# Two decode layers with a key and value cache: every cache load as two halves of 64 partitions, on two DMA queues

## The chip, the cores and the metric

The kernel runs on one core of a Trainium2 chip. The metric is the device time of one execution in microseconds (us); smaller is better. A difference of under about 0.2% (some 5 us) can't be told from no change here.

## What is computed

The reference takes one token for each of two sequences (x is 2 x 1 x 576) through attention, a gated MLP, attention and the MLP again, with the same weights and the same cache both times, all in float32. There are 32 heads of 128 dimensions and 8192 cached positions.

```python
def _A_ref(x, k_cache, v_cache, wq, wo):
    q = (x @ wq).reshape(B, Sq, H, Dh).transpose(0, 2, 1, 3)
    scores = jnp.einsum("bhqd,bhkd->bhqk", q, k_cache) * (Dh ** -0.5)
    p = _softmax(scores, axis=-1)
    o = jnp.einsum("bhqk,bhkd->bhqd", p, v_cache)
    return o.transpose(0, 2, 1, 3).reshape(B, Sq, H * Dh) @ wo
def _B_ref(x, w_gate, w_up, w_down):
    return (_gelu(x @ w_gate) * (x @ w_up)) @ w_down
x = x + _A_ref(_layernorm(x), k_cache, v_cache, wq, wo)
x = x + _B_ref(_layernorm(x), w_gate, w_up, w_down)
x = x + _A_ref(_layernorm(x), k_cache, v_cache, wq, wo)
x = x + _B_ref(_layernorm(x), w_gate, w_up, w_down)
```

Each head's keys are 4 MB, and so are its values. For 2 sequences and 32 heads that is 537 MB in a layer, nearly all of which is read from DRAM twice, once for each layer. This is far more than the weights.

## The kernel before, in words

The attention of a layer goes item by item. An item is two heads of one sequence (30 items, `PAIRS`), or at the end of the list a single head (4 items, `SINGLE`). A load of the keys or values of a pair is 8 MB: 128 partitions with 128 cached rows, that is 64 KB in one run, each. Partitions 0 to 63 hold the first head of the pair and 64 to 127 the second. Layer 0 takes the items from first to last and layer 1 from last to first, so that what is still held from the end of layer 0 need not be loaded again.

The tile `space` is most of the on-chip memory. `Arena` is its planner: six slots of 32 KB a partition, so places for three pairs, and behind them a ring of four smaller places for weights. All loads stand in one list, in the order of `plan_first`, `plan_mlp` and `plan_second`. A load is written into the program as soon as its place is free there: `done` frees a place and calls `pump`, which issues from the head of the list. So the order of the loads is fixed, and each DMA instruction waits at its place in its engine's program until the last reader of the memory is done. Keys and values alternate: keys of item n+1, values of item n.

All cache loads but two go through `load` (line 165), which issues one DMA on SP's queue (L168). `cache`, `half`, `one` and `several_parts` call it. `by_rows` (L233) and all loads of weights (L257 to L322) issue their DMAs on SP themselves. ScalarE issues eight small loads of x at the start (L143), and one of the two stores at the end (L1201).

Work on an item's keys: VectorE multiplies them with the query (L743), GpSimd adds the halves of each row (L772), and VectorE sums them into scores (L775). VectorE and TensorE find the peak (L799 to L809), and ScalarE computes the weights (L824, L832). Work on the values: TensorE multiplies them with the weights (L913), except for the last two parts, which VectorE weighs (L880) and GpSimd folds (L883) before TensorE adds them in (L891). The place of an item's keys is freed by L775, that of its values by L913 and, last, L891. TensorE broadcasts the next item's query (L658) once VectorE has begun on the present one, and ScalarE scales a pair's result (L955). At the start of layer 1 ScalarE also copies queries (L740), so that GpSimd can multiply some rows (L759), and sums some rows itself (L765). L615 is the products with `wq`.

Of the kernel before, what the change touches and what calls it, by code (L numbers as in the profile page):

```python
# [15 lines left out]
P = 128  # L16
# [8 lines left out]
JC = 16  # L25
# [37 lines left out]
ITEMS = [Item(b, h, 2) for h in range(0, H - 2, 2) for b in range(B)]  # L63
# [62 lines left out]
def decode_layers(ctx, tc, x_in, kc, vc, wq, wo, wg, wu, wd, out):  # L126
    nc = tc.nc
# [12 lines left out]
    for c in range(4):  # L140
        for s in range(2):
            lo = 32 * c + s * B
# [16 lines left out]
    def part_at(at, n):  # L159
        return space[:, at:at + n]  # L160
# [4 lines left out]
    def load(at, n, src, lo, hi):  # L165

        t = part_at(at, (hi - lo) * PART).rearrange("p (j d) -> p j d", d=DH)
        nc.sync.dma_start(t, ITEMS[n].source(src)[:, lo * JC:hi * JC, :])  # L168

    def cache(key, src, n, slots=None):  # L170

        parts = ITEMS[n].parts

        def make():
            at = arena.pair(key) if slots is None else arena.slots(key, slots, parts)
            if at is None:
                return False
            load(at[0], n, src, 0, parts)
            ready[key] = dict(enumerate(map(part, at)))
            places[key] = at  # L180
            return True

        queue.append(make)

    def half(key, src, n, k, slot):

        def make():
            at = arena.slots(key, (slot,), 4, k)
            if at is None:
                return False  # L190
            load(at[0], n, src, k, k + 4)
            ready.setdefault(key, {}).update((k + i, part(a)) for i, a in enumerate(at))
            return True

        queue.append(make)

    def one(key, src, n, k, where):

        def make():
            at = arena.ring((key, k), PART) if where is None else arena.take((key, k), places[where[0]][where[1]], PART)  # L200
            if at is None:
                return False
            load(at, n, src, k, k + 1)
            ready.setdefault(key, {})[k] = part(at)
            return True

        queue.append(make)
# [250 lines left out]
    for b in range(B):  # L458
        rows = ident.rearrange("p (c v i r) -> p i r v c", c=4, v=4, i=2)[:, :, :, b, :]
# [769 lines left out]
```

## Time and profile before

| | |
|---|---|
| Median of 3 runs | 2681.43 us (2681.32 to 2682.24) |
| The profiled execution: its own time | 2681.31 us |
| Its span in the profile | 2679.5 us |
| Bytes read from DRAM | 1152.39 MB |
| VectorE busy | 1992.6 us (74%) |
| GpSimd busy | 1560.5 us (58%) |
| TensorE busy | 880.8 us (33%) |
| ScalarE busy | 165.7 us (6%) |
| SP's DMA queue, share of 16 DMA engines | 99.8% |

In the profile SP's queue is q1 and ScalarE's is q10. "SPq" and "ACTq" are the issuing instructions of SP and ScalarE, in which an engine spends its time only until the DMA is handed over. L numbers are lines of the kernel before; after the change lines behind 168 are two higher.

### The profile page before, as it was taken

The page shows a single profiled execution, that of the slowest core. Times are in us where ns is not written, and L with a number is a line of the kernel's source. Part 1 is how long each engine was busy: PE and PEld are TensorE (multiplying, and loading weights), DVE is VectorE, ACT ScalarE, POOL GpSimd, SP SyncE. Part 2 cuts the span into 40 slices and gives each one's busy share as a digit, 9 for nine tenths or more (in the row PEclk, how much of TensorE's full clock was granted, in tenths as well). Part 3 has the DMA queues.
Part 4 walks back from the last instruction along what each step waited for, and adds up shares of the span by engine and source line. Part 5 has one row for each costly group of instructions (what it writes and reads, how often), then busy time and mean ns, then how long its engine had stood idle before and what let it go on. Part 6 is the DMA issues. An engine that isn't in the chain of part 4 may idle for free.

```text
span 2679.5 us, 15405 instructions
## 1 busy us (share of the span) xinstructions
PE 880.8 (33%) x6198; PEld 268.7 (10%) x6198; DVE 1992.6 (74%) x907; ACT 165.7 (6%) x792; POOL 1560.5 (58%) x411
## 2 busy tenths in 40 slices
PE   1313332232223233334663323223222323332346
PEld 0000000000000000011221000000000000000022
DVE  4877888888788888867038778888888888888740
ACT  0000000000000000001026000000000000000000
POOL 2546676667667666744028457666766666676620
PEclk8666655665665566566986665566566556655678
DMA  9999999999999999999999999999999999999998
GB/s 423 437 429 434 436 434 432 431 436 433 431 434 434 434 433 432 436 428 427 417 417 431 436 433 434 434 430 434 435 432 432 436 434 433 431 437 434 428 430 385
DMA packets 29207, 1153.39 MB, mean 430 GB/s; under 512 B 3256, under 2 KB 3280, under 8 KB 4048
## 3 DMA queue, kind: packets, MB, share of 16 engines
q1 hardware_dynamic: 29096, 1152.40, 99.8%
q8 instruction: 48, 0.79, 0.1%
q14 instruction: 23, 0.19, 0.0%
q10 hardware_dynamic: 40, 0.01, 0.0%
HBM read 1152.39 MB, written 0.00 MB: 430 GB/s over the span
## 4 chain that ended last, share of the span: by engine, by line
DMA 67%; DVE 19%; PE 8%; POOL 2%; ACT 2%; issue 1%; another core or an unknown queue 0%; SPq 0%; POOLq 0%; ACTq 0%; DVEq 0%
DMA space<-in_A_k_cache_dram 59%; DVE space L743 17%; PE acc L891 3%; DMA space<-in_B_w_down_dram 2%; DMA space<-in_B_w_gate_dram 2%; POOL space L772 2%; DVE scores L775 2%; PE bank L658 1%; DMA space<-in_A_v_cache_dram 1%; DMA space<-in_B_w_up_dram 1%; PE bank L809 1%; ACT prz L832 1%; PE acc L913 1%; DMA space<-in_A_wo_dram 1%; PE bank L845 1%
## 5 line engine op out<-in xcount | busy, mean ns | idle before, releaser
L772 POOL TENSOR_TENSOR space<-space 128x3072 f32<-128x3072 f32 (+4 forms) x221 | 1128.4, 5106 | 459.1 <-DVE space L743 330.7
L743 DVE TENSOR_TENSOR space<-space,bank 128x6144 f32<-128x6144 f32 (+4 forms) x223 | 1111.9, 4987 | 344.7 <-DMA space<-in_A_k_cache_dram 273.7
L775 DVE TENSOR_REDUCE scores<-space 128x48 f32<-128x3072 f32 (+4 forms) x223 | 568.7, 2550 | 92.1 <-POOL space L772 92.1
L913 PE MATMUL acc<-space,prz 128*16 128x512 f32 (+1 forms) x3312 | 510.1, 780 | 357.9 <-DMA space<-in_A_v_cache_dram 346.4
L883 POOL TENSOR_TENSOR space<-space 128x2048 f32<-128x2048 f32 x147 | 398.0, 2708 | 392.3 <-DVE space L880 376.8
L658 PE MATMUL bank<-qsb,few 4*64 4x128 f32 (+1 forms) x256 | 46.1, 436 | 894.8 <-DVE space L743 887.1
L880 DVE TENSOR_TENSOR space<-space,bank 128x4096 f32<-128x4096 f32 x49 | 216.6, 4421 | 1.7
L913 PEld LDWEIGHTS acc<-space,prz 128*16 128x16 f32 (+1 forms) x3312 | 108.7, 117 | 742.0 <-issue 449.7
L824 ACT ACTIVATE nbs<-bank 128x2 f32<-128x2 f32 (+1 forms) x68 | 11.6, 171 | 2010.4 <-PE bank L809 1957.1
L658 PEld LDWEIGHTS bank<-qsb,few 4*64 4x64 f32 (+1 forms) x256 | 20.6, 201 | 914.2 <-DVE space L743 897.4
L580 POOL TENSOR_TENSOR rstd<-ve,few 128x1 f32<-128x1 f32 x4 | 2.2, 551 | 171.3 <-DVE ve L578 171.3
L891 PE MATMUL acc<-space,few 128*16 128x512 f32 x98 | 92.6, 1048 | 0.0
L801 PE MATMUL bank<-ident,m 128*1 128x128 f32 x68 | 20.7, 305 | 196.1 <-DVE m L799 195.9
L936 PE MATMUL bank<-few,wide 128*32 128x4 f32 (+1 forms) x272 | 20.9, 200 | 170.1 <-DVE wide L928 170.1
L1153 DVE STREAM_TRANSPOSE gu<-acc 128x288 f32<-128x288 f32 x4 | 1.9, 484 | 92.6 <-ACT acc L1151 92.6
L832 ACT ACTIVATE prz<-scores,nbs 64x128 f32<-64x128 f32 (+1 forms) x128 | 50.7, 396 | 11.7 <-POOL prz L822 8.9
L765 ACT ACTIVATE space<-space 128x128 f32<-128x128 f32 x164 | 48.4, 297 | 19.5 <-DVE space L743 16.5
L809 PE MATMUL bank<-m,few 1*128 1x2 f32 (+1 forms) x136 | 39.0, 353 | 28.1 <-DVE m L807 28.1
L584 DVE TENSOR_TENSOR x<-bank,x 128x144 f32<-128x144 f32 x4 | 1.2, 308 | 59.4 <-PE bank L1186 39.7
L927 DVE TENSOR_TENSOR acc<-acc,few 128x512 f32<-128x512 f32 x34 | 23.5, 691 | 29.2 <-PE acc L913 29.2
L936 PEld LDWEIGHTS bank<-few,wide 128*32 128x32 f32 x272 | 19.1, 154 | 216.0 <-issue 211.0
L955 ACT ACTIVATE oT<-bank,rinv 32x8 f32<-32x8 f32 x108 | 28.1, 260 | 190.1 <-PE bank L936 189.1
(105 smaller groups left out, 495.8 us busy)
## 6 DMA issues: line engine op xcount, KB each, us to landing
space<-in_A_v_cache_dram SPq DMA_DIRECT2D x7, 4096.0 KB
space<-in_A_k_cache_dram SPq DMA_DIRECT2D x6, 4096.0 KB
space<-in_B_w_gate_dram SPq DMA_DIRECT2D x9, 1152.0 KB
space<-in_B_w_up_dram SPq DMA_DIRECT2D x9, 1152.0 KB
space<-in_B_w_down_dram SPq DMA_DIRECT2D x8, 1152.0 KB
space<-in_A_wq_dram SPq DMA_DIRECT2D x9, 1024.0 KB
space<-in_A_wo_dram SPq DMA_DIRECT2D x2, 4608.0 KB
space<-in_A_k_cache_dram SPq DMA_DIRECT2D x4, 2048.0 KB
```

The lines of the kernel that those rows point to most:

```text
L658: nc.tensor.matmul(qb[n][to, :], pick[32 * c:32 * c + 4, r:r + 1].to_broadcast([4, P // it.heads]), qsb[32 * c:32 * c + 4, (h % 4) * DH:(h ...
L743: nc.vector.tensor_tensor(out=u[:, :r, :], in0=t[:, :r, :], in1=qb[n].unsqueeze(1).to_broadcast([P, r, DH]), op=ALU.mult)
L765: nc.scalar.activation(u[:, j, :], u[:, j, :], AF.Copy, accum_out=S[n][:, base(n, k) + j:base(n, k) + j + 1])
L772: nc.gpsimd.tensor_tensor(out=half, in0=half, in1=u[:, :r, DH // 2:], op=ALU.add)
L775: nc.vector.tensor_reduce(out=S[n][:, base(n, k):base(n, k) + own_rows(n, k, m)], in_=prod.pop((n, k)), axis=AX.X, op=ALU.add)
L809: nc.tensor.matmul(mT[n][:, :heads], ones[0:1, :], m1[:, :heads], start=True, stop=True)
L832: nc.scalar.activation(pr[at, lo:].rearrange("p (g e) -> p g e", e=4)[:, 0:it.rows // 2 * it.heads:2 * it.heads, :], s[at, :it.rows].rearr ...
L880: nc.vector.tensor_tensor(out=t, in0=t, in1=share.unsqueeze(2).to_broadcast([P, rows, DH]), op=ALU.mult)
L883: nc.gpsimd.tensor_tensor(out=t[:, :rows - less], in0=t[:, :rows - less], in1=t[:, less:rows], op=ALU.add)
L891: nc.tensor.matmul(accumulator(n)[0:16, :], owner[:, 8 * ITEMS[n].b:8 * ITEMS[n].b + 16], part_at(arena.live[key, lo][0], 4 * DH), start=F ...
L913: nc.tensor.matmul(accumulator(n)[32 * c:32 * c + m, :], pr[:, at:at + m], t[g // 4][:, g % 4 * 4:g % 4 * 4 + 4, :].rearrange("p j d -> p ...
L936: nc.tensor.matmul(po[lo:lo + 32, i, :c], t[:, i::GH], of[:, :c], start=True, stop=True)
```

## The change

```diff
     def load(at, n, src, lo, hi):

         t = part_at(at, (hi - lo) * PART).rearrange("p (j d) -> p j d", d=DH)
-        nc.sync.dma_start(t, ITEMS[n].source(src)[:, lo * JC:hi * JC, :])
+        rows = ITEMS[n].source(src)[:, lo * JC:hi * JC, :]
+        for engine, p in ((nc.sync, 0), (nc.scalar, P // 2)):
+            engine.dma_start(t[p:p + P // 2], rows[p:p + P // 2])
```

Each of the 141 loads that go through `load` becomes two DMAs: partitions 0 to 63 on SP's queue and partitions 64 to 127 on ScalarE's. Both wait for the same readers of the place, each in its own engine's program. `by_rows` and the weights stay as they were.

At the start ScalarE's program before, behind its loads of x, had the table load, the scaled queries (`qsb`) and then the first items' softmax (`nbs`, `prz`):

```order
L143 DMA x<-in_A_x_dram 2x144 x8
L989 ACT_TABLE_LOAD
L989 ACTIVATE qsb<-acc,rstd 128x256 x2
L824 ACTIVATE nbs<-bank_124 128x2
L832 ACTIVATE prz,few<-scores,nbs 64x32x4 x2
```

Now it reads, at the same place:

```order
L143 DMA x<-in_A_x_dram 2x144 x8
L170 DMA space<-in_A_k_cache_dram 64x16384 x2
L170 DMA space<-in_A_v_cache_dram 64x16384
L991 ACT_TABLE_LOAD
L991 ACTIVATE qsb<-acc,rstd 128x256 x2
L170 DMA space<-in_A_k_cache_dram 64x16384
L826 ACTIVATE nbs<-bank_125 128x2
L834 ACTIVATE prz,few<-scores,nbs 64x32x4 x2
```

Three halves of loads stand ahead of `qsb`, the first of which waits for no reader.

In the middle of a layer, ScalarE's program for two items (`oT` is the scaled result of a pair) was:

```order
L824 ACTIVATE nbs<-bank_124 128x2
L832 ACTIVATE prz,few<-scores,nbs 64x32x4 x2
L824 ACTIVATE nbs<-bank_124 128x2
L832 ACTIVATE prz,few<-scores,nbs 64x32x4 x2
L955 ACTIVATE oT<-bank_124,rinv 32x8 x4
```

and is now:

```order
L826 ACTIVATE nbs<-bank_125 128x2
L834 ACTIVATE prz,few<-scores,nbs 64x32x4 x2
L170 DMA space<-in_A_k_cache_dram 64x16384
L170 DMA space<-in_A_v_cache_dram 64x16384
L826 ACTIVATE nbs<-bank_125 128x2
L834 ACTIVATE prz,few<-scores,nbs 64x32x4 x2
L170 DMA space<-in_A_k_cache_dram 64x16384
L957 ACTIVATE oT<-bank_125,rinv 32x8 x4
L170 DMA space<-in_A_v_cache_dram 64x16384
```

The halves stand between an item's weights and the next item's.

At the start of layer 1, where ScalarE computes more, it had, from the scaled queries on:

```order
L989 ACTIVATE qsb<-acc,rstd 128x256 x2
L740 COPY qs<-bank 128x128
L765 ACTIVATE space,scores<-space 128x128 x12
L730 COPY space<-prz 128x264
L765 ACTIVATE space,scores<-space 128x128 x12
```

and has now:

```order
L991 ACTIVATE qsb<-acc,rstd 128x256 x2
L170 DMA space<-in_A_k_cache_dram 64x2048
L742 COPY qs<-bank 128x128
L767 ACTIVATE space,scores<-space 128x128 x12
L732 COPY space<-prz 128x264
L767 ACTIVATE space,scores<-space 128x128 x7
L170 DMA space<-in_A_k_cache_dram 64x4096
L767 ACTIVATE space,scores<-space 128x128 x5
L170 DMA space<-in_A_k_cache_dram 64x2048 x2
```

Here halves of small loads stand ahead of the copy of the query, and within ScalarE's sums.

## The prediction

> **What bounds the kernel now.** I read the page from the top: the span, the forty slices, the queues, the chain of work that ended last.
>
> ```profile
> span 2679.5 us, 15405 instructions
> GB/s 423 437 429 434 436 434 432 431 436 433 431 434 434 434 433 432 436 428 427 417 417 431 436 433 434 434 430 434 435 432 432 436 434 433 431 437 434 428 430 385
> DMA packets 29207, 1153.39 MB, mean 430 GB/s; under 512 B 3256, under 2 KB 3280, under 8 KB 4048
> q1 hardware_dynamic: 29096, 1152.40, 99.8%
> q10 hardware_dynamic: 40, 0.01, 0.0%
> DMA 67%; DVE 19%; PE 8%; POOL 2%; ACT 2%; issue 1%; another core or an unknown queue 0%; SPq 0%; POOLq 0%; ACTq 0%; DVEq 0%
> ```
>
> The reader is to see that most slices stand at 430 to 437 GB/s and that one queue, q1, keeps the 16 DMA engines busy for 99.8% of the span. The chain shows DMA for 67% and VectorE for 19%, but the queue is full during VectorE's share too: VectorE sits in the chain only because it frees the place of a later load. The two attention stages alone, in a table of busy time by stage (last columns: granted clock, DMA share, GB/s):
>
> ```profile
> 24.00:1253.00 1229.00, 364.94 (x2077) 103.87 (x2081) 985.27 (x380) 57.12 (x228) 767.44 (x181) 0.60 1.00 433
> 1463.00:2576.00 1113.00, 328.25 (x1858) 91.95 (x1858) 909.70 (x347) 48.14 (x202) 724.79 (x169) 0.59 1.00 433
> ```
>
> Both run at 433 GB/s with a DMA share of 1.00. So the time is bytes divided by rate, and only two things can move it: a change of the rate, or a moment in which the queue runs dry. How near it is to dry, the chain in order of time and SP's issues show:
>
> ```profile
> 461.99 29.05 DMA space<-in_A_k_cache_dram
> 491.04 0.02 issue
> 491.07 6.57 DVE space L743
> ```
>
> ```profile
> 442.25 0.33 SPq L168 DMA_DIRECT2D space<-in_A_v_cache_dram  x1
> 461.99 0.33 SPq L168 DMA_DIRECT2D space<-in_A_k_cache_dram  x1
> 482.20 0.33 SPq L168 DMA_DIRECT2D space<-in_A_v_cache_dram  x1
> ```
>
> A pair's load is 128 partitions of 64 KB, 8.39 MB, and takes 8.39 / 0.433 = 19.4 us. The keys issued at 461.99 land at 491.04, 29.05 us later, so they stood 9.7 us behind the load before them. The values issued at 482.20 start when these keys have landed, 8.8 us later. **The lead is about 9 us.**
>
> **The change, part by part.** What goes through `load` is taken from the table of DMA issues, whose sizes are in KB:
>
> ```profile
> space<-in_A_v_cache_dram SPq DMA_DIRECT2D x7, 4096.0 KB
> space<-in_A_k_cache_dram SPq DMA_DIRECT2D x6, 4096.0 KB
> space<-in_A_k_cache_dram SPq DMA_DIRECT2D x4, 2048.0 KB
> space<-in_A_v_cache_dram SPq DMA_DIRECT2D x2, 2048.0 KB
> space<-in_A_k_cache_dram SPq DMA_DIRECT2D x4, 1024.0 KB
> space<-in_A_v_cache_dram SPq DMA_DIRECT2D x1, 3072.0 KB
> space<-in_A_v_cache_dram SPq DMA_DIRECT2D x1, 1024.0 KB
> space<-in_A_k_cache_dram SPq DMA_DIRECT2D x58
> space<-in_A_v_cache_dram SPq DMA_DIRECT2D x58
> ```
>
> The last two rows carry no size; they are the 116 pair loads, 973.1 MB by the shapes in the code. The others are 54.5 + 12.6 + 8.4 = 75.5 MB. Together 141 loads move 1048.6 MB, which at 433 GB/s is **2422 us**. The rest of the queue's 1152.40 MB, and the two ends of the kernel, are not touched.
>
> *Issue.* 141 DMAs more are issued, all on ScalarE. SP's cost 0.33 us each by the rows above; the only ones that ScalarE issues in a row are those of x:
>
> ```profile
> 1.04 14.66 ACTq L143 DMA_DIRECT2D x<-in_A_x_dram  x8
> ```
>
> That is 1.83 us each, waits included, so 47 to 258 us of ScalarE's time. ScalarE is busy for 165.7 us and waits for most of the rest, as its largest wait shows:
>
> ```profile
> ACT nbs L824 <- PE bank L809: 1957.1, 63, 41.0
> ```
>
> I cost the issues at nothing: ScalarE's 1957 us of waiting and the lead of 9 us hide them. If that cover were gone, a half would land up to 1.5 us late.
>
> *Waits.* In the middle of a layer the halves stand in ScalarE's program in the order in which SP issued them among ScalarE's own work:
>
> ```profile
> 460.18 0.17 ACT L824 ACTIVATE nbs<-bank 128x2 f32<-128x2 f32 x1 [37.49 <-PE bank L809]
> 461.19 0.18 ACT L832 ACTIVATION_READ_ACCUMULATOR prz<-scores,nbs 64x1 f32 x1
> 468.37 1.08 ACT L955 ACTIVATE oT<-bank,rinv 32x8 f32<-32x8 f32 x4 [6.99 <-PE bank L936]
> ```
>
> The softmax ends at 461.37 and the keys are issued at 461.99. The scaled result follows at 468.37, the values at 482.20. No half waits behind ScalarE's work, nor does that work wait behind a half: nothing.
>
> At the start of layer 1 this does not hold:
>
> ```profile
> 1382.31 0.27 ACT L740 COPY qs<-bank 128x128 f32<-128x128 f32 x1 [0.43 <-PE bank L658]
> 1382.65 2.51 POOL L759 TENSOR_TENSOR space<-space,qs 128x512 f32<-128x512 f32 x2 [11.62 <-ACT qs L740]
> 1388.40 9.19 SPq L168 DMA_DIRECT2D space<-in_A_k_cache_dram  x4
> 1394.24 0.75 DVE L775 TENSOR_REDUCE scores<-space 128x9 f32<-128x576 f32 x1 [2.58 <-POOL space L772]
> ```
>
> SP issues at 1388.40 the load whose second half now stands ahead of the copy at 1382.31. So the copy comes 6.1 us later, GpSimd's L759 with it, and VectorE's L775, which frees the next places. If the queue has 6 us of work, the cost is 0; if it has none, 6 us, and twice that if the next such place adds as much. I take 5 us and keep 0 to 12.
>
> At the start of the kernel ScalarE's first half is issued behind x, at about 15.7 us, and runs beside the second part of `wq`:
>
> ```profile
> 28.03 9.85 PE L615 MATMUL acc<-space,xt 128*4 128x512 f32 x72 [1.64 <-DVE ve L578]
> 44.62 6.55 DVE L743 TENSOR_TENSOR space<-space,bank 128x6144 f32<-128x6144 f32 x1 [16.60 <-DMA space<-in_A_k_cache_dram]
> ```
>
> The first keys land at 44.62, so `wq` was in at about 44.6 - 19.4 = 25.2; now it is in 9.7 us later at most (half of a load), at 34.9. TensorE is on the first part, 40 of the 72 products, until 28.0 + 5.5 = 33.5, so the products end some 1.4 us later than 37.9. VectorE waits for the keys until 44.62 anyway: nothing.
>
> *The rate.* This decides. The packets under 512 B are the ends of DMAs: the issue table has 202 loads by SP, and 202 x 16 + 8 x 2 (x, two rows each) + 2 x 4 (the stores, four rows each) = 3256, exactly the page's number. So a load of 128 rows is dealt to 16 engines, and I expect the same for a half of 64 rows, with four rows for each engine where a whole load has eight. A row of 64 KB takes an engine 65.5 KB / 27.1 GB/s = 2.42 us. With both queues full, an engine takes a row of one half, then a row of the other; all 16 start with SP's half. **At one moment all 16 write to the same 64 partitions.** Can 64 partitions take 433 GB/s? No row shows it: each load of before fills 128 partitions, and none of the slices gives a partition more than 437 / 128 = 3.4 GB/s. If the engines are the limit, the halves cost nothing (or, should two queues close the gaps between rows, the best slice's 437 instead of 433 gains 22 us). If the partitions' side is the limit, each half goes at half of the rate while it has the engines alone, and the cost is up to another 2422 us. [...] I take the partitions' side, since the change doubles the load on exactly that and the rows show no spare there. The engines won't be exactly in step; with nothing to size it, I take 7% of the collision off (an estimate), and keep none and a quarter for the case's own range: 2422 x 0.93 = **2252 us**.
>
> [...]
>
> Sum: the profiled execution took 2681.31 us (span 2679.5 and 1.8 around it), within 0.1 us of the median of 2681.43. 2681 + 2252, and the 5 us of layer 1 vanish because the queue is then far longer: **4930 us**, by itself 4500 to 5110.
>
> **The rivals.**
> 1. *The engines are the limit; halves don't collide.* The place is every moment with a row of each half in flight, and it decides if 64 partitions can take 433 GB/s. For it speaks that the rate is the same in both stages and that q1 alone fills the engines; against it only that no row shows a fuller partition. The two queues then share the engines and the bytes set the time: 2681 + 5 (layer 1) = 2686 us, 2681 to 2693. About half of it is within 0.2% (the 5 us that a measurement can tell from no change). [...]
> 2. *Collision, but engines fall out of step.* If one engine writes to one half while its neighbour writes to the other, neither is slowed. With half of the time in collision: 2681 + 0.5 x 2422 = 3890 us. [...]
> 3. *Two queues close the gaps.* 1048.6 MB at 437 instead of 433 GB/s is 2400 instead of 2422 us: 2659 us. Against it: a share of 99.8% leaves little to close.
>
> That the change does not do what it says is excluded by the program's order: ScalarE's program has the halves.
>
> **How the numbers follow.** Collision in step 0.58, out of step 0.12, no collision 0.27, gaps closed 0.03. Slower is 0.58 + 0.12 + half of 0.27 = 0.83, the same 0.14, faster 0.03. The two collisions hold only 0.70, so the range has to reach down to the case without one: 2680 to 5150 us, wide because the price is either nothing or the cache's whole time again.
>
> **What would show it.** q10 with about 524 MB. If the forecast is right, slices in attention at 215 to 240 GB/s with the DMA share still near 1, and 415 to 430 in the weights' slices; a pair's load about 37 us; VectorE's L743 waiting for keys most of the time. If the first rival is right, slices stay at 433 and L743's waits stay as they were. A middle rate in attention shows the second. It would prove me wrong in the waits if ScalarE's L740 is not late at the start of layer 1, or if ScalarE's halves are issued microseconds behind SP's in the middle of a layer.

## The result, and the profile after

The changed kernel takes **5012.38 us** (median of 4 runs, 4953.01 to 5052.14) against 2681.42 us before (2681.32 to 2682.24). The ratio is 1.852, 95% interval 1.844 to 1.861. The changed kernel's four times fall into two pairs; the ratio is of the lower pair (4953.01 and 4979.99 us, median 4966.5), and the profile is of a run of the upper pair, which took 5044.77 us.

The page after, in the lines that answer to those of before (of the groups, VectorE's product of the keys, whose last columns are idle time before it and what ended most of that):

```profile
span 5043.0 us, 15864 instructions
GB/s 241 213 211 210 214 209 216 216 216 217 216 215 216 216 217 222 224 235 255 239 381 227 215 216 224 237 222 220 228 230 215 217 221 222 224 223 234 216 216 342
DMA packets 31467, 1153.43 MB, mean 229 GB/s; under 512 B 5513, under 2 KB 5537, under 8 KB 6305
q1 hardware_dynamic: 20072, 628.11, 52.6%
q10 hardware_dynamic: 11320, 524.31, 47.1%
L745 DVE TENSOR_TENSOR space<-space,bank 128x6144 f32<-128x6144 f32 (+4 forms) x223 | 1111.9, 4987 | 1831.9 <-DMA space<-in_A_k_cache_dram 1714.7
```

Before, the same group read:

```profile
L743 DVE TENSOR_TENSOR space<-space,bank 128x6144 f32<-128x6144 f32 (+4 forms) x223 | 1111.9, 4987 | 344.7 <-DMA space<-in_A_k_cache_dram 273.7
```

The bytes are the same, and now q10 carries 524 MB of them. The two queues' shares add up to 99.7%: the engines count as busy as before (99.8%), but move half as much in that time (229 GB/s in the mean, before 430). Almost the only fast slices are those with weights. VectorE's product now waits 1715 us for keys, before 274. By stage (the columns are those of the table by stage in the prediction):

```profile
100.00:2200.00 2100.00, 300.04 (x1710) 84.84 (x1710) 870.10 (x309) 44.61 (x187) 692.45 (x155) 0.55 1.00 216
2900.00:4900.00 2000.00, 295.80 (x1636) 84.90 (x1636) 857.44 (x321) 44.60 (x187) 685.96 (x161) 0.54 1.00 223
```

```profile
2520.00:2590.00 70.00, 43.44 (x594) 16.49 (x588) 5.36 (x24) 1.42 (x4) 0.55 (x1) 0.98 1.01 421
```

216 and 223 GB/s in attention at a DMA share of 1.00, and 421 where whole loads of weights of 128 partitions run on SP alone. Packets under 512 B went from 3256 to 5513, which is 141 x 16 more and one: each half is dealt to 16 engines. In the middle of a layer both queues are issued at the same moment (SP's rows, then ScalarE's):

```profile
602.33 0.47 SPq L170 DMA_DIRECT2D space<-in_A_k_cache_dram  x1
622.49 0.47 SPq L170 DMA_DIRECT2D space<-in_A_v_cache_dram  x1
```

```profile
602.33 0.50 ACTq L170 DMA_DIRECT2D space<-in_A_k_cache_dram  x1
622.49 0.50 ACTq L170 DMA_DIRECT2D space<-in_A_v_cache_dram  x1
```

So here neither the issue (0.50 us) nor ScalarE's own work holds a half back. What is lost is rate.

### The profile page after: what moved, and what is told of

Read it like the earlier page. It is cut to its first block, busy times and chain, and to the rows that moved or that the text cites. A ratio compares the mean times of both kernels' runs of the same rounds, so it can differ in the third digit from the quotient of the medians.

```text
span 5043.0 us, 15864 instructions
## 1 busy us (share of the span) xinstructions
PE 887.7 (18%) x6198; PEld 273.5 (5%) x6198; DVE 1993.1 (40%) x907; ACT 165.1 (3%) x792; POOL 1555.5 (31%) x411
## 2 busy tenths in 40 slices
DMA packets 31467, 1153.43 MB, mean 229 GB/s; under 512 B 5513, under 2 KB 5537, under 8 KB 6305
## 4 chain that ended last, share of the span: by engine, by line
another core or an unknown queue 59%; DVE 19%; PE 11%; DMA 8%; POOL 1%; issue 1%; ACT 1%; ACTq 0%; DVEq 0%; POOLq 0%; SPq 0%
DVE space L745 13%; PE acc L915 8%; DVE space L882 4%; DMA space<-in_A_v_cache_dram 2%; DMA space<-in_B_w_down_dram 1%; DMA space<-in_A_k_cache_dram 1%; DVE scores L777 1%; DMA space<-in_A_wo_dram 1%; POOL space L774 1%; PE acc L893 1%; PE bank L660 1%; DMA space<-in_A_wq_dram 1%; DMA space<-in_B_w_up_dram 1%; ACT prz L834 0%
## 5 line engine op out<-in xcount | busy, mean ns | idle before, releaser
L761 POOL TENSOR_TENSOR space<-space,qs 128x512 f32<-128x512 f32 x23 | 29.3, 1276 | 43.0 <-ACT qs L742 31.2
L811 PEld LDWEIGHTS bank<-m,few 1*128 1x128 f32 x136 | 33.3, 302 | 69.5 <-DVE m L809 51.3
```

Of the source, the lines that this page charges most:

```text
L761: nc.gpsimd.tensor_tensor(out=u[:, rows:every, :], in0=t[:, rows:every, :], in1=q.unsqueeze(1).to_broadcast([P, every - rows, DH]), op=ALU ...
L811: nc.tensor.matmul(mT[n][:, :heads], ones[0:1, :], m1[:, :heads], start=True, stop=True)
```

## The experiments

Four explanations of the lost rate were set against each other. **S**: the two halves of the partitions are the two ways in, each for the work of eight engines. **Q**: switching between two queues with every row costs. **N**: any DMA to 64 partitions is slow. **E**: the engines alone are the limit (then there would be no loss).

The diffs show the lines that matter. A line with a minus is one of the changed kernel or of the run shown before. Where the DMA engines are idle for part of the time, "GB/s while busy" is the rate divided by the DMA share.

### One queue

```diff
-        for engine, p in ((nc.sync, 0), (nc.scalar, P // 2)):
+        for engine, p in ((nc.sync, 0), (nc.sync, P // 2)):
```

> Both halves of each load on SP's queue, one behind the other; ScalarE issues none. S (the partitions' side: 64 partitions of one half take 217 GB/s, whoever issues): the halves never overlap, 2681 + 2422 = about 5100 us, at least 4900. Q (alternating between two queues, row by row, is what costs): one queue has nothing to alternate, so 2681 to 2700 us.

Measured: 5262.32 us (two runs, 5225.06 to 5299.59). In the first attention:

```profile
100.00:2200.00 2100.00, 291.38 (x1644) 84.14 (x1644) 817.57 (x291) 42.46 (x178) 651.42 (x147) 0.54 1.00 208
```

Q is out: without a second queue it is slower still, 208 GB/s instead of 216. And it is slower than S had it: a half alone doesn't go at half of 433, 216.5, but at 208.

### Two queues, split by rows

```diff
+        m = (hi - lo) * JC // 2
+        for engine, r in ((nc.sync, 0), (nc.scalar, m)):
+            engine.dma_start(t[:, r:r + m], rows[:, r:r + m])
```

> Two DMAs for each load on the two queues as in the change, but each fills all 128 partitions with half of the cached rows. S: no collision, 433 GB/s, 2681 to 2700 us. Q: each engine still alternates between the queues with every row, now of 32 KB, so as slow as the change or slower, 5000 us and more.

Measured: 2697.32 us, ratio 1.0056 (1.0039 to 1.0073).

```profile
100.00:1100.00 1000.00, 287.86 (x1602) 80.44 (x1606) 818.33 (x294) 43.52 (x182) 653.65 (x148) 0.59 1.00 431
```

As many DMAs on the same two queues, and 431 GB/s. So neither the second queue nor the number of DMAs costs the rate; what is left is which partitions a DMA fills. The 15 us that remain are taken apart further down.

### Half of the bytes: the lower 64 partitions, or the middle 64

```diff
+        loads.append(n)
+        p, q = (0, P) if len(loads) <= 3 else (0, P // 2)
+        nc.sync.dma_start(t[p:q], rows[p:q])
```

The second kernel has `(P // 4, 3 * P // 4)` in place of `(0, P // 2)`.

> Left out: the upper 64 partitions of every cache load behind the first three (the old bytes stay there); SP alone issues the lower half. Half of the cache's bytes, so 1152 - 512 = 641 MB. S: 64 partitions at 217 GB/s need as long for half of the bytes as 128 for all, so about 2680 us, 2650 to 2750. E (the engines were the limit and 64 partitions take 433): the loads need half of the time, and VectorE's 1993 us of work become the bound, 2050 to 2200 us.

> As the run with the lower half only, but it is partitions 32 to 95 that are loaded: also 64 partitions and the same bytes, 32 of each half. S (what is limited is a fixed way into each half of the partitions): both ways are used, 433 GB/s, so VectorE bounds it, 2050 to 2200 us. N (any transfer to 64 partitions goes at half of the rate, since a partition takes no more than 3.4 GB/s or a small transfer is dealt out badly): 2650 to 2750 us.

Measured (one run each): 2810.82 us with the lower half, 2413.28 us with the middle. The first attention of the lower half, then that of the middle:

```profile
100.00:1100.00 1000.00, 283.42 (x1525) 78.56 (x1525) 775.07 (x279) 41.26 (x173) 615.69 (x140) 0.59 1.00 206
```

```profile
100.00:1100.00 1000.00, 327.90 (x1911) 106.66 (x1911) 912.19 (x342) 52.80 (x214) 718.07 (x166) 0.60 0.59 243
```

This pair settles most. The lower half needs longer for half of the bytes than the old kernel for all: 206 GB/s at a share of 1.00. The middle is as many partitions, bytes and DMAs, and its source is as contiguous, yet its DMA engines are busy for only 0.59 of the time: 243 / 0.59 = 412 GB/s while busy. E falls by the first and N by the second. S was right in kind, but its 2650 to 2750 us for the lower half were too low, since the half goes at 206 and not at 217. My 2050 to 2200 us for the middle were too low as well: VectorE, busy for 912 of these 1000 us, sets the pace in attention, but the stage around the border of the layers comes on top, where from 1080 to 1300 us it is busy for only 105.

One rival these two leave: in a pair's load a partition and its place in DRAM go together, so the place in DRAM could be what is slow. The old kernel's loads of single heads speak against it. Each reads the 4 MB of one head in one piece, as the load of a lower half does, but into 128 partitions (old kernel, a stretch in which only such loads run):

```profile
1198.00:1250.00 52.00, 17.68 (x89) 6.61 (x89) 36.52 (x34) 5.20 (x16) 22.15 (x12) 0.61 1.00 430
```

430 GB/s, against 206 for such a piece in partitions 0 to 63. So the limit goes with the partitions.

### Finer than halves: 32 partitions around the border, and 32 at the bottom

```diff
-        p, q = (0, P) if len(loads) <= 3 else (0, P // 2)
+        p, q = (0, P) if len(loads) <= 3 else (48, 80)
```

The control has `(0, 32)`.

> Left out: all but partitions 48 to 79 of every cache load behind the first three; SP alone issues, 16 partitions of each half, two rows for each engine if dealt as before. VectorE bounds the time (2400 us or a little less, as with the middle half), so the rate is read while the DMA engines are busy: GB/s divided by the DMA share. S (the ways in are the two halves, each for eight engines): 433 while busy. [...]

> The control to the run with partitions 48 to 79: partitions 0 to 31 alone behind the first three loads, the same bytes. S: all 16 engines on the lower half, 206 while busy. [...]

Measured: 2413.47 and 2415.30 us. Partitions 48 to 79, then 0 to 31:

```profile
100.00:1100.00 1000.00, 326.32 (x1911) 106.85 (x1911) 912.24 (x342) 52.77 (x214) 717.87 (x166) 0.61 0.58 121
```

```profile
100.00:1100.00 1000.00, 323.02 (x1911) 105.92 (x1911) 912.04 (x342) 52.85 (x214) 718.29 (x166) 0.61 0.58 122
```

121 / 0.58 = 209 and 122 / 0.58 = 210 GB/s while busy. S in its plain form missed: it had 433 for 48 to 79, which lies in both halves, and this range is as slow as 0 to 31. Of the contiguous ranges that were loaded alone, 32 to 95 went at 412 GB/s, and 0 to 63, 0 to 31 and 48 to 79 at 206 to 210. What sets apart the fast one is not shown: no load of 32 partitions alone was fast, so these two runs don't part the place of a range from its size, and no run here shows single engines.

### Even and odd partitions

```diff
-        for engine, p in ((nc.sync, 0), (nc.scalar, P // 2)):
-            engine.dma_start(t[p:p + P // 2], rows[p:p + P // 2])
+        for engine, p in ((nc.sync, 0), (nc.scalar, 1)):
+            engine.dma_start(t[p::2], rows[p::2])
```

> SP loads the even partitions of each cache load, ScalarE the odd ones: 64 partitions for each DMA again, but each spread over both halves. S in its plain form (the two halves 0 to 63 and 64 to 127 are the ways in, each for 217 GB/s): no collision, 2681 to 2700 us. [...]

Measured: 2693.51 us (one run).

```profile
100.00:1100.00 1000.00, 289.75 (x1610) 81.23 (x1614) 817.43 (x294) 43.53 (x182) 652.25 (x148) 0.59 1.00 433
```

Two DMAs of 64 partitions on two queues at the full 433 GB/s: the shape of the change without its loss, and within the 2681 to 2700 us that S had. To see whether the second queue is what makes it fast, the even ones alone, on SP (and the odd ones left out):

```diff
-        p, q = (0, P) if len(loads) <= 3 else (48, 80)
-        nc.sync.dma_start(t[p:q], rows[p:q])
+        p, q = (0, 1) if len(loads) <= 3 else (0, 2)
+        nc.sync.dma_start(t[p::q], rows[p::q])
```

> Left out: the odd partitions of every cache load behind the first three; SP alone issues the even ones, so one DMA of 64 partitions with a step of two and no second queue. [...]

Measured: 2414.71 us (one run).

```profile
100.00:1100.00 1000.00, 318.96 (x1911) 104.92 (x1911) 912.23 (x342) 52.81 (x214) 717.85 (x166) 0.61 0.60 244
```

244 / 0.60 = 407 GB/s while busy, so the DMA is fast by itself, and the second queue is not what makes it so. How it is dealt to the engines stays open.

### The middle on one queue, the rest on the other

```diff
+        for engine, p, q in ((nc.sync, P // 4, 3 * P // 4), (nc.scalar, 0, P // 4), (nc.scalar, 3 * P // 4, P)):
+            engine.dma_start(t[p:q], rows[p:q])
```

> SP loads partitions 32 to 95 of each cache load, ScalarE partitions 0 to 31 and 96 to 127 as two more DMAs; all bytes are loaded. S (a fixed way into each half of the partitions): SP's part meets no limit (9.7 us for a pair), ScalarE's two DMAs each lie in one half and go at half of the rate if nothing is beside them (9.7 us each), so 1.5 times as long for the cache: 2681 + 0.5 x 2422 = about 3900 us, down to 3300 if engines on one half meet engines on the other. N (any DMA to fewer partitions is slow in proportion): the two quarters at a quarter of the rate, 19.4 us each, and the middle 19.4: about 7500 us.

Measured: 5264.85 us (one run).

```profile
100.00:2200.00 2100.00, 294.96 (x1645) 84.49 (x1645) 835.41 (x297) 42.41 (x178) 666.52 (x150) 0.54 0.99 210
```

A miss: 210 GB/s, no better than one queue with halves. In the same stretch SP's queue, which carries the middle, shows:

```profile
q1 hardware_dynamic: 4238, 222.17, 47.1%
```

That is 222.17 MB / (0.471 x 2100 us) = 225 GB/s while this queue's rows are in work, where the middle by itself has 412. So the middle is held up when rows of the two quarters run beside it, which S left out. An explanation would be that rows of the quarters hold up nearly every row of the middle; that was not tested. N, which had 7500 us, is no better.

### What two queues cost without a collision

Three kernels take the 15 us of the split by rows and the 12 us of even and odd apart. The first splits by rows, but only the loads of a pair:

```diff
+        m = (hi - lo) * JC // 2
+        halves = ((nc.sync, 0, m), (nc.scalar, m, 2 * m)) if hi - lo == 8 else ((nc.sync, 0, 2 * m),)
+        for engine, r, e in halves:
+            engine.dma_start(t[:, r:e], rows[:, r:e])
```

> As the run split by rows over all 128 partitions on two queues (2697.3 us), but only the 116 loads of a pair are split; the smaller ones go whole on SP. If the copy of the query that ScalarE makes late at the start of layer 1 costs what the stage 1400 to 1470 us lost (426 to 388 GB/s over 70 us, 6 us), this takes 2690 to 2692 us. If the loss is in the pieces of 32 KB alone, it stays at 2696 to 2698.

Measured: 2690.96 us, ratio 1.0034 (1.0021 to 1.0047). 6 us less, as the late copy had it; but all small loads are whole here, so this does not part the copy from the other small halves.

The second splits all loads by rows, with both DMAs on SP:

```diff
-        for engine, r in ((nc.sync, 0), (nc.scalar, m)):
+        for engine, r in ((nc.sync, 0), (nc.sync, m)):
```

> The split by rows over all 128 partitions, with both DMAs on SP's queue. Rows of 32 KB instead of 64, no second queue, no issue by ScalarE. If shorter rows cost the 2 GB/s (433 to 431) of the attention stages, 2690 to 2693 us; if the second queue cost them, 2681 to 2684.

Measured: 2692.05 us, ratio 1.0039 (1.0024 to 1.0053). The first attention runs at 431 GB/s again, so the 2 GB/s go with the rows of 32 KB and not with the second queue. The third splits the pairs' loads into even and odd:

```diff
+        halves = ((nc.sync, 0, 2), (nc.scalar, 1, 2)) if hi - lo == 8 else ((nc.sync, 0, 1),)
+        for engine, p, step in halves:
+            engine.dma_start(t[p::step], rows[p::step])
```

> Even partitions on SP, odd ones on ScalarE, for the 116 loads of a pair alone; the smaller loads go whole on SP. The run with all loads split so took 2693.5 us at 433 GB/s in the attention stages. If its 12 us are ScalarE's late copy and the small loads around the layers' border, this is within 0.2% of before, 2680 to 2686 us; if two queues cost something in the middle of a layer, 2690 or more.

Measured: 2686.24 us, ratio 1.0019 (1.0009 to 1.0028), 7 us less than with all loads split and at the upper edge of the 2680 to 2686 us. Two thirds of what is left lies at the start (before, then this kernel):

```profile
24.00:60.00 36.00, 11.59 (x82) 2.85 (x82) 16.60 (x9) 2.12 (x3) 8.65 (x3) 0.75 1.01 437
```

```profile
24.00:60.00 36.00, 12.13 (x82) 2.90 (x82) 13.28 (x8) 2.12 (x3) 5.99 (x2) 0.77 0.96 408
```

```profile
SPq L171 <- DMA space<-in_A_wq_dram: 17.3, 1, 17.3
```

The first keys, issued at 10.80 us before, wait here 17.3 us for the DMA of `wq`, and the queue runs dry: 36 us x (1 - 408/437) = 2.4 us, against 3.8 us between the spans of the two profiled executions (2679.5 and 2683.3). No version with two queues beats the old kernel.

## Why the prediction was right

The range, 2680 to 5150 us, held both outcomes, so that the time fell into it says little. What counts is the choice that was made and its price.

**What bounds it** held: in attention the share stays at 1.00, and the time moved with the rate.

**The rate**, on which all hung, was taken rightly: collision, and slower by 1.85. Which partitions a DMA fills sets the rate (206 GB/s for the lower half, 412 for the middle half), and both halves in turn on one queue go at 208. The queues' rows do take turns: of 16 rows from 672.6 to 677.4 us 13 are SP's, of 15 from 677.6 to 682.4 us 12 are ScalarE's. From 702.6 to 707.4 us all 16 rows are ScalarE's (the other packets are those under 512 B):

```profile
DMA packets 23, 1.05 MB, mean 218 GB/s; under 512 B 7, under 2 KB 7, under 8 KB 7
q10 hardware_dynamic: 18, 1.05, 103.9%
q1 hardware_dynamic: 5, 0.00, 0.1%
```

But the form I gave it was too simple. 64 partitions as such are not slow (32 to 95 went at 412), and two halves of 217 GB/s each don't explain 48 to 79, which lies in both and went at 209. What sets the rate of a range was not shown; the kernel with the middle beside the rest stays unexplained too.

**Its size** came out near by luck, by two errors that cancel. The term of the sum was 2252 us; measured it is 4966.5 - 2681.42 = 2285 by the two lower runs, and 5012.38 - 2681.42 = 2331 by the median of all four. I had a half alone at 216.5 GB/s, so 2422 us for full collision; a half alone goes at 206 to 208, and one queue shows the price, 5262.32 - 2681.95 = 2580 us. And I took 7% off with nothing to size it; two queues take 2285 against 2580, 11% off. What wins this back was not tested.

**Issue and waits in the middle of a layer** cost nothing, as the issues at 602.33 on both queues show.

**The start of layer 1** was right in mechanism. The copy of the query waits behind a half. ScalarE is idle for 7.07 us before it, where that was 0.43, so the copy comes 6.6 us later, where I had 6.1 (changed kernel):

```profile
2619.86 0.49 ACTq L170 DMA_DIRECT2D space<-in_A_k_cache_dram  x1
2620.39 0.27 ACT L742 COPY qs<-bank 128x128 f32<-128x128 f32 x1 [7.07 <-PE acc L617]
```

What it costs, the collision hides in the changed kernel, whose DMA share stays at 1.01 there (2620 to 2700 us). Even and odd show it, with all loads split:

```profile
1360.00:1400.00 40.00, 23.96 (x224) 6.57 (x224) 9.99 (x14) 5.07 (x29) 4.47 (x4) 0.94 0.97 397
1400.00:1470.00 70.00, 31.62 (x168) 10.16 (x168) 51.30 (x65) 42.67 (x267) 50.83 (x42) 0.67 0.96 388
```

Shares of 0.97 and 0.96, and 397 and 388 GB/s, where before had 1.01, 415 and 426: the queue runs dry there. Leaving the small loads whole took 7.3 us off (2693.51 to 2686.24), the late copy and the other small halves together. I had 5, with 0 to 12.

**The start of the kernel** I had at nothing, and that step was wrong. I had `wq` in at 34.9 us at the latest. In the changed kernel the products that need its second part start at 53.97, after a wait for it:

```profile
53.97 5.82 PE L617 MATMUL acc<-space,xt 128*4 128x512 f32 x32 [13.30 <-DMA space<-in_A_wq_dram]
```

I had let ScalarE's half cost `wq` at most the 9.7 us of its bytes at full rate, and so left the collision out of this step: from 24 to 100 us the changed kernel moves 212 GB/s. In the pairs' even and odd kernel, without collision, the start costs 2.4 us, since the first keys wait for `wq` there: a small miss, in a wait that I had not read from the program.

**The rivals.** No collision (2686 us, 2681 to 2693) is out for these halves. Even and odd halves of all loads, which keep the late copy and have no collision, take 2693.51 us, the upper end of that. That the pairs' alone take 2686.24 is chance, for the late copy, which made up the 5 us, is gone there. Engines out of step (3890 us) supposed that neither half is slowed while both are written to. The trace of the changed kernel shows otherwise: from 134.4 to 139.2 us 9 rows are SP's and 7 ScalarE's, and the rate is 218 GB/s, the same as with all 16 in one half:

```profile
DMA packets 16, 1.05 MB, mean 218 GB/s; under 512 B 0, under 2 KB 0, under 8 KB 0
q1 hardware_dynamic: 9, 0.59, 56.6%
q10 hardware_dynamic: 7, 0.46, 44.0%
```

Closed gaps: nothing of it was seen, no attention stage with two queues went above 433.

## What to carry to other kernels

Whole loads and halves alike were dealt to 16 engines (by the packets under 512 B, 3256 and 5513), and yet which partitions a DMA filled set its rate. Before cutting a load by partitions, ask which ones move at the same time: 0 to 63 went at 206 GB/s, 32 to 95 at 412 alone and at 225 beside the other two quarters, every second one at 407. A second queue gained nothing where one kept the engines busy (431 and 433 GB/s, before 433), and DMAs on ScalarE also put its own work behind their waits (a copy came 6.6 us later).

## What the runs showed of the hardware that was not expected

- The slow ranges alone don't go at half of 433, 216.5, but at 206 to 210 GB/s, in four kernels (one queue, lower half, 0 to 31, 48 to 79). That is 3 to 5% below the half.
- A DMA to every second partition is not slow: 433 GB/s together with its twin, 407 while busy alone.
- A DMA of partitions 32 to 95 loses its rate beside DMAs of the other two quarters: 225 GB/s while busy instead of 412.
- Rows of 32 KB instead of 64 cost 2 GB/s of 433, on one queue as on two.
